# A new instruction order for a fused state-space and gated-MLP kernel: six idle matmuls fewer, all reloads on one queue

## The chip, the cores and the metric

The kernel runs on one core of a Trainium2 chip. The core has five engines that run their own instruction lists and wait for each other by semaphores: TensorE (PE, with its weight loads listed as PEld), VectorE (DVE), ScalarE (ACT), GpSimd (POOL) and SyncE (SP), which here only issues transfers; ACT and POOL issue a few too. Operands lie in SBUF, matmuls write to eight PSUM banks. The metric is the device time of one execution in microseconds (us), lower is better. Of the kernel before there are three timed runs, with a median of 218.31, and one profiled execution.

## The reference

The input is one sequence x of 2048 tokens by 512 channels. After a layer norm over the channels, two branches work on the same normed xn, and the result is x plus both.

```python
xn = layernorm(x)                                   # over D = 512, no gain
# branch A: per channel d a long convolution, its filter from 128 complex modes
dt = exp(log_dt)[:, None]
P  = exp(dt * (A_re + 1j*A_im))[:, :, None] ** l    # l = 0..2047
K  = einsum("dn,dnl,dn->dl", C, P, dt * B).real     # filter, D x 2048
y  = irfft(rfft(pad(xn.T)) * rfft(pad(K)))[:, :2048].T + xn * Dskip
# branch B: gated MLP, F = 1792
h  = sigmoid(xn @ w_gate) * (xn @ w_up)
return x + y + h @ w_down
```

The positions l are rounded to bf16 in the reference, and the kernel follows that.

## The kernel before

**Stages.** The 2048 tokens are 16 tiles of 128 rows. Tile by tile the layer norm takes statistics (DVE, lines 535 to 537, or ACT, lines 528 to 530, by the table `ON_ACT`), POOL takes the power for 1/sqrt (line 491), and DVE or ACT applies it (549, 544). The first four tiles are transposed on PE with the identity (line 558) and evicted to `xnT` (line 293); the other twelve go out to memory and come back by a transposing DMA.

Branch B runs in four groups of 512 tokens. For each of 14 blocks of F there are four gate matmuls (line 1020), a sigmoid on ACT (1029), four up matmuls (1035) and a product on DVE (1050). `UEV` lists the products for which ACT first copies the up projection out of PSUM (line 1046, `us_sb`); for the others DVE reads PSUM. Then four times 14 down matmuls (1079).

Branch A makes powers of the modes (ACT 649, DVE 658 and 660, cast on the way by POOL's DMAs, 654), and from them, for four chunks of 128 channels, two tables by complex multiplies (DVE 715 to 721, ACT 768 and DVE 773 and 774). A chunk's tables are multiplied on PE (799), evicted (the helper `copy`, on ACT as line 293 or on DVE as line 291, by `ON_DVE`), re-sorted on PE (820), evicted to the filter table and given the skip weight (DVE 832). Meanwhile xn goes through a first transform (PE 677) to scratch memory `z_scr`. Then, in two passes over half of the channels and, in each, four pairs of frequency units: reload of z, second transform (PE 868), filter spectrum (PE 883), products (DVE 888 and 892), in the second pass sums (899 to 903), the inverse transform's first half (PE 915 in the first pass, 925 in the second), eviction, store to `v_scr`. `v_scr` is three tensors: all units of pass 0 (`v_scr_97`), units 0 to 5 of pass 1 (`v_scr_98`) and units 6 and 7 of pass 1 (`v_scr_99`), so that each can be reloaded as soon as it is whole. Each is reloaded in four parts, for token tiles 0 to 3, 4 to 7, 8 to 11 and 12 to 15. The inverse transform's second half (PE 988) gives y of a tile, and DVE adds it to x plus the MLP's result (1003), or, for the last group, adds x to the sum that PE made of both (1099). The result is stored two tiles at a time.

A correction for rounded positions, the skip-row terms, is made by small steps (PE 947, DVE 952 to 959, PE 965, ACT 967), stored to `r_scr`, and added to two rows of x by POOL's accumulating DMAs (1066). POOL's line 1116 adds x to finished MLP tiles by DMA.

**What sets the order.** Nothing is ordered at run time: every piece of work is added to a plan (`pl.add`) with an engine, a cost, dependencies and a priority, and the list `ORDER`, written out in the file, says in which sequence the 981 pieces are emitted. Each engine runs its part of that sequence strictly in order; a piece that waits holds back all that follow on its engine. SP's transfers are pieces of that list as well, and one that waits holds back the later ones. PSUM banks and small buffers are dealt out along the same sequence.

**Around the change.** Before the first data PE runs idle matmuls on a zeroed tile, `keep_warm` (line 513): one block of eight and three blocks from `WARM`. The first loads are tiles 0 to 3 of x, log_dt and A (`l_pa`), the identity (`l_id`), B and C (`l_pbc`), then the weights. The reloads of `v_scr` are issued by SP, but for two of the last tensor:

```python
lds.append(dma("ACT" if n == 2 and t % 4 else "SP", vall[16 * u0:16 * u1, t // 2, p], v_v[t // 2],
               deps=v_st[n] + table_free + z_free * p, prio=20 + n + 0.01 * t, pkt=2048, hv=0.9)(64 * KB * (u1 - u0)))
```

Of the kernel before, what the change touches and what calls it, by code (L numbers as in the profile page):

```python
# [13 lines left out]
ACT = mybir.ActivationFunctionType  # L14
# [35 lines left out]
WARM = (4, 4, 3)  # L50
# [17 lines left out]
KB = 1024  # L68
# [114 lines left out]
def _consts():  # L183
# [22 lines left out]
UEV = (2, 4, 5, 7, 11, 13, 14, 15, 16, 17, 18, 19, 23, 24, 25, 28, 29, 30, 31, 32, 33, 34, 35, 36, 37, 38, 39, 40, 41, 42, 43, 44, 47, 53, 54, 55,)  # L206
ON_DVE = (95, 96, 97, 109, 118, 194, 232, 242, 375, 376, 379, 495, 508, 513, 598,)
ON_ACT = (3, 6, 8, 9, 10, 11,)
ORDER = [
# [42 lines left out]

class _Op:
    __slots__ = ("alt", "tab", "eng", "cost", "fn", "prio", "acq", "rel", "dma", "left", "users", "ready", "start", "done", "seq", "mode")
# [69 lines left out]
def kernel(  # L324
# [39 lines left out]
    ident = const.tile([128, 128], BF, name="ident")  # L364
# [811 lines left out]
```

## Time and profile before

| | |
|---|---|
| timed runs | 218.31 us median (217.55 to 221.57) |
| profiled execution | 218.46 us |
| its span, first to last instruction | 216.6 us |
| PE busy | 203.7 us, 94% |
| DVE busy | 196.2 us, 91% |
| ACT busy | 177.7 us, 82% |
| POOL busy | 33.7 us, 16% |
| moved by DMA | 42.40 MB, mean 196 GB/s |
| granted PE clock | 1.00 |

Matmuls overlap in their records, so PE's busy time says that it works, not how well. In a group, busy over count is what one instruction adds, since the mean duration also holds the overlap with the next. The end of an instruction's idle time is put down to what released it.

### The profile page before, as it was taken

What the parts mean: (1) busy time and instruction counts of PE and PEld (TensorE: products, weight loads), DVE (VectorE), ACT (ScalarE), POOL (GpSimd) and SP (SyncE); (2) the same over time, 40 slices, a digit from 0 to 9 for tenths busy, and PEclk for the clock granted to TensorE, in tenths of its full rate; (3) what the DMA queues carried; (4) which work ended last, traced back from release to release, by engine and by line L of the source; (5) the groups of instructions that cost most, each with busy time, mean ns of one, the idle gap of its engine ahead of it and who ended that gap; (6) DMA issues with size and microseconds to landing.
All of it is one profiled execution on the core that took longest, in us unless ns stands there. A gap on an engine that the chain in (4) does not pass through costs nothing.

```text
span 216.6 us, 5697 instructions
## 1 busy us (share of the span) xinstructions
PE 203.7 (94%) x2202; PEld 103.3 (48%) x2228; DVE 196.2 (91%) x433; ACT 177.7 (82%) x365; POOL 33.7 (16%) x63
## 2 busy tenths in 40 slices
PE   7899999999999999999999999999979999998593
PEld 2474444443443454445556555644544555433252
DVE  4899899999999999999999999999869999991484
ACT  4799999999999999899999999975668999960000
POOL 3200543563110231000000006100000005100000
PEclk9999999999999999999999999999999999999999
DMA  5999907995659841596448464915974879689844
GB/s 165 387 413 425 293 5 120 189 129 145 97 194 233 226 140 59 124 268 198 125 160 258 132 207 88 173 40 166 322 232 131 267 247 297 110 248 254 211 172 178
DMA packets 41757, 42.40 MB, mean 196 GB/s; under 512 B 8953, under 2 KB 35202, under 8 KB 41602
## 3 DMA queue, kind: packets, MB, share of 16 engines
q1 hardware_dynamic: 36978, 36.98, 55.5%
q0 software_dynamic: 4512, 4.73, 14.1%
q10 hardware_dynamic: 240, 0.33, 0.6%
q8 instruction: 17, 0.28, 0.5%
q14 instruction: 10, 0.08, 0.1%
HBM read 25.24 MB, written 12.07 MB: 172 GB/s over the span
## 4 chain that ended last, share of the span: by engine, by line
PE 38%; DVE 28%; ACT 24%; DMA 4%; issue 3%; POOL 0%; DVEq 0%; SPq 0%; ACTq 0%; POOLq 0%
PE bank L1020 8%; ACT big L293 8%; PE bank L883 7%; PE bank L1035 7%; DVE hT_sb L1050 5%; PE bank L1079 4%; DVE big L715 4%; DVE big L716 4%; ACT hT_sb L1029 3%; PE bank L513 3%; ACT big L649 3%; DMA big<-v_scr 2%; ACT us_sb L1046 2%; ACT big L544 2%; PE bank L868 2%
## 5 line engine op out<-in xcount | busy, mean ns | idle before, releaser
L293 ACT ACTIVATE big<-bank 128x512 bf16<-128x512 f32 (+2 forms) x149 | 82.7, 688 | 9.3 <-PE bank L799 3.8
L1020 PE MATMUL bank<-xnT,wg_sb 128*128 128x512 bf16 (+1 forms) x237 | 53.1, 361 | 2.0 <-ACT xnT L293 0.6
L1035 PE MATMUL bank<-xnT,wu_sb 128*128 128x512 bf16 x211 | 53.5, 379 | 0.5
L1079 PE MATMUL bank<-wd_sb,hT_sb 128*128 128x512 bf16 (+1 forms) x232 | 49.9, 366 | 0.4
L1029 ACT ACTIVATE hT_sb<-bank 128x512 bf16<-128x512 f32 x56 | 35.1, 687 | 1.4 <-PE bank L1020 1.3
L1020 PEld LDWEIGHTS <-wg_sb 128*128 128x128 bf16 x244 | 23.4, 98 | 25.8 <-issue 4.0
L1079 PEld LDWEIGHTS <-hT_sb 128*128 128x128 bf16 x238 | 22.8, 98 | 25.4 <-issue 1.9
L1035 PEld LDWEIGHTS <-wu_sb 128*128 128x128 bf16 x224 | 20.7, 98 | 27.0 <-issue 4.3
L715 DVE TENSOR_TENSOR big<-big 128x1024 bf16<-128x1024 bf16 (+4 forms) x40 | 26.6, 666 | 0.1
L716 DVE TENSOR_TENSOR big<-big 128x1024 bf16<-128x1024 bf16 (+4 forms) x40 | 26.5, 662 | 0.0
L1046 ACT ACTIVATE us_sb<-bank 128x512 bf16<-128x512 f32 x36 | 24.8, 721 | 0.8 <-DVE hT_sb L1050 0.8
L888 DVE TENSOR_TENSOR big<-big 128x2048 bf16<-128x2048 bf16 x16 | 19.4, 1218 | 0.1
L883 PE MATMUL bank<-big 128*128 128x256 bf16 x160 | 19.3, 273 | 0.0
L883 PEld LDWEIGHTS <-big 128*128 128x128 bf16 x160 | 15.3, 98 | 4.1 <-issue 0.8
L654 POOL DMA_DIRECT2D big<-big x24 | 13.0, 546 | 25.5 <-DVE big L660 25.3
L720 DVE TENSOR_TENSOR big<-big 128x512 bf16<-128x512 bf16 (+4 forms) x40 | 16.4, 410 | 0.0
L721 DVE TENSOR_TENSOR big<-big 128x512 bf16<-128x512 bf16 (+4 forms) x40 | 16.4, 409 | 0.0
L293 ACT ACTIVATE big<-big 128x256 bf16<-128x256 bf16 x33 | 16.3, 527 | 0.0
L768 ACT ACTIVATE sq_sb<-big 128x256 bf16<-128x256 bf16 (+2 forms) x20 | 14.9, 747 | 1.1 <-DVE big L721 1.1
L1050 DVE TENSOR_TENSOR hT_sb<-hT_sb,us_sb 128x512 bf16<-128x512 bf16 x36 | 14.9, 417 | 0.6 <-ACT us_sb L1046 0.5
L1050 DVE TENSOR_TENSOR hT_sb<-hT_sb,bank 128x512 bf16<-128x512 bf16 x20 | 13.3, 679 | 0.0
L1003 DVE TENSOR_TENSOR big<-bank,glu_sb 128x512 bf16<-128x512 f32 x8 | 5.0, 682 | 8.4 <-PE bank L988 8.4
(96 smaller groups left out, 219.8 us busy)
## 6 DMA issues: line engine op xcount, KB each, us to landing
big<-c_E SPq DMA_DIRECT2D x16, 320.0 KB, 4.2
z_scr<-big SPq DMA_DIRECT2D x16, 256.0 KB, 3.1
big<-z_scr SPq DMA_DIRECT2D x16, 256.0 KB, 5.2
v_scr<-big SPq DMA_DIRECT2D x16, 256.0 KB, 2.9
big<-big POOLq DMA_DIRECT2D x24, 128.0 KB, 2.8
big<-in_A_u_dram SPq DMA_DIRECT2D x4, 512.0 KB, 10.3
big<-v_scr SPq DMA_DIRECT2D x4, 512.0 KB, 4.4
wu_sb<-in_B_w_up_dram SPq DMA_DIRECT2D x2, 896.0 KB, 10.1
```

What stands on the lines that cost most here:

```text
L293: nc.scalar.activation(out=get(out), in_=get(in_), func=ACT.Identity)
L715: V.tensor_tensor(out=wide(outp), in0=wide(lo), in1=mre, op=ALU.mult)
L716: V.tensor_tensor(out=wide(tb()), in0=wide(lo), in1=mim, op=ALU.mult)
L720: V.tensor_tensor(out=outp[:, :, 0], in0=outp[:, :, 0], in1=tb()[:, :, 1], op=opr)
L883: T.matmul(bank(sk[kt == NKT - 1])[:, DW * c:DW * c + DW], es()[:, c, kt, :], kT[p][:, kt, :], start=kt in (0, NKT - 1), stop=kt >= NKT - 2)
L888: V.tensor_tensor(out=pp()[:, :, 0:4, :], in0=xx()[:, :, 0, :].unsqueeze(2).to_broadcast([128, 2, 4, DW]), in1=kb().unsqueeze(1).to_broadc ...
L1020: T.matmul(bank(sl)[:, c0:c1], w_at(w, CUT_G, kt, k), xnT[:, grp, kt, c0:c1], start=(kt == 0), stop=(kt == KT - 1))
L1029: S.activation(out=hT_sb[:, hs.idx, k % 2, :], in_=bank(sl), func=ACT.Sigmoid)
L1035: T.matmul(bank(sl), w_at(wu_sb, CUT_U, kt, k), xnT[:, grp, kt, :], start=(kt == 0), stop=(kt == KT - 1))
L1046: S.activation(out=us_sb[:, us.idx, :], in_=bank(sl), func=ACT.Identity)
L1050: V.tensor_tensor(out=h(), in0=h(), in1=us_sb[:, us.idx, :] if on else bank(sl), op=ALU.mult)
L1079: T.matmul(bank(po)[:, 0:c[1] - c[0]], hT_sb[:, hts[k // 2].idx, k % 2, jj * 128:(jj + 1) * 128], wd_sb[:, k, c[0]:c[1]], start=first and ...
```

## The change

Four edits, and what follows from the last. The identity is loaded ahead of `l_pa` in SP's queue. The first block of idle matmuls has nine instead of eight, and of the three further blocks (4, 4, 3) two remain (2, 2). All reloads of `v_scr` are issued by SP. `ORDER` is replaced throughout, and with it the tables that say which engine does a piece: `UEV` has 37 entries for 36, `ON_DVE` 16 for 15, `ON_ACT` five for six. The computation is the same.

```diff
-WARM = (4, 4, 3)
+WARM = (2, 2)
...
-UEV = (2, 4, 5, 7, 11, 13, 14, 15, 16, 17, 18, 19, 23, 24, 25, 28, 29, 30, 31, 32, 33, 34, 35, 36, 37, 38, 39, 40, 41, 42, 43, 44, 47, 53, 54, 55,)
-ON_DVE = (95, 96, 97, 109, 118, 194, 232, 242, 375, 376, 379, 495, 508, 513, 598,)
-ON_ACT = (3, 6, 8, 9, 10, 11,)
+UEV = (0, 1, 3, 10, 12, 15, 16, 18, 19, 20, 21, 22, 24, 25, 26, 27, 28, 29, 30, 31, 32, 33, 34, 35, 36, 37, 38, 39, 40, 41, 42, 44, 46, 48, 49, 54, 55,)
+ON_DVE = (94, 95, 96, 108, 117, 180, 190, 193, 382, 498, 531, 540, 597, 599, 871, 873,)
+ON_ACT = (2, 4, 8, 11, 15,)
 ORDER = [
-    0, 24, 25, 2, 22, 21, 1, 3, 4, 7, 34, 26, 29, 6, 5, 8, 10, 35, 36, 37, 43, 44, 30, 31, 20, 27, 38, 28, 32, 40, 41, 23,
+    1, 28, 21, 22, 29, 2, 0, 3, 23, 24, 33, 4, 7, 6, 30, 34, 25, 35, 42, 43, 39, 20, 31, 32, 26, 27, 45, 36, 40, 44, 41,
...
+    l_id = load("SP", ident[:], cten["ident"].ap(), 32 * KB)
     l_pa = load("SP", par[:, 0:3, :], A_par[:, 0:3, :], 384 * KB, pkt=3072)
-    l_id = load("SP", ident[:], cten["ident"].ap(), 32 * KB)
...
-    warm = [keep_warm(8, -10)]
+    warm = [keep_warm(9, -10)]
...
-            lds.append(dma("ACT" if n == 2 and t % 4 else "SP", vall[16 * u0:16 * u1, t // 2, p], v_v[t // 2],
+            lds.append(dma("SP", vall[16 * u0:16 * u1, t // 2, p], v_v[t // 2],
```

In the emitted programs the new order shows at these places, among others. All 13 idle matmuls stand ahead of the first transposes; before it was 16 and then 3. In the last chunk of the filter (the last 128 of line 799), PE's work between lines 799 and 820 was 12 matmuls of line 1020 and 4 of 1035, and is 8, 4 and 16 of line 868; the four evictions there were one on ACT and three on DVE, and are all on ACT; between lines 820 and 883 there were 16 of line 868, 4 of line 1020 and 8 of line 947, and are 4 of line 1035. After the last 16 of line 925 PE had 8 matmuls of line 1035 and 28 of line 1079 ahead of the first line 988, and has 12 of line 1035, 4 of line 965, 4 of line 1020 and the 28. Line 988 then came as 12, 14 of line 1079, 22, and comes as 16, 14 of line 1079, 18. SP's end of the list is, before and after (tile parts by their first pair of tiles):

```
before: store 99, store 99, reload 98 t2, 98 t4, 99 t4, 98 t0, 99 t0, 98 t6      ACT: 99 t2, 99 t6
after:  reload 98 t4, store 99, store 99, reload 98 t2, 98 t6, store r_scr, 99 t4, 99 t6, 99 t2, 98 t0, 99 t0
```

82 rows, old and new, of the table ORDER are left out of this document.

## The prediction

> **What bounds the kernel now.** First the page's busy shares, then the same in six stretches cut where the kind of work changes. The columns of the second are the stretch, its length, and the busy time (with the instruction count) of PE, PE's weight loads, DVE, ACT and POOL, then the granted clock, the DMA share and GB/s.
>
> ```profile
> span 216.6 us, 5697 instructions
> ...
> PE 203.7 (94%) x2202; PEld 103.3 (48%) x2228; DVE 196.2 (91%) x433; ACT 177.7 (82%) x365; POOL 33.7 (16%) x63
> ```
>
> ```profile
> 0.00:27.00 27.00, 24.31 (x129) 12.72 (x132) 21.91 (x54) 22.58 (x42) 6.28 (x19) 1.00 0.95 337
> 27.00:151.87 124.87, 123.29 (x1407) 60.78 (x1422) 123.97 (x287) 119.17 (x251) 23.97 (x40) 1.00 0.63 151
> 151.87:163.20 11.33, 9.85 (x255) 6.24 (x256) 8.61 (x23) 7.43 (x15) 0.00 (x0) 1.00 0.83 260
> 163.20:191.32 28.12, 27.54 (x290) 13.94 (x292) 27.78 (x47) 26.38 (x55) 3.46 (x4) 1.00 0.78 219
> 191.32:203.11 11.79, 8.91 (x56) 3.93 (x59) 4.08 (x9) 2.17 (x4) 0.00 (x0) 1.00 0.95 246
> 203.11:216.60 13.49, 9.80 (x74) 5.67 (x70) 9.81 (x17) 0.00 (x0) 0.00 (x0) 1.00 0.50 177
> ```
>
> DVE is the bound: from 27 to 151.87 it idles 0.90 us, from 163.20 to 191.32 0.34 us. It loses time in four places: the head, 151.87 to 163.20 (2.72 idle, the last filter chunk's way through PE and ACT), 191.32 to 203.11 (7.71, the store and reload of the last products) and the end (3.68, from the first of the final adds at 203.11). PE has few holes either. So a new order can gain only by less DVE work or by closing those four.
>
> **The change, part by part.** The profiled run took 218.46 us, span 216.6 plus 1.86 around it; the median shown is 218.31. I work from 218.46. Where I count instructions, they are those of the two programs as built, each at busy time over count of its group.
>
> *Head.* These are rows of the chain of waits and of the timeline.
>
> ```profile
> 1.46 6.20 PE bank L513 x16
> 6.39 0.63 ACT L595 ACTIVATE big<-big 128x512 bf16<-128x512 bf16 x1 [0.40 <-DMA big<-in_A_par_dram]
> 7.92 1.09 ACT L293 ACTIVATE xnT<-bank 128x512 bf16<-128x512 bf16 x2 [0.90 <-PE bank L558]
> 8.76 0.81 PE L513 MATMUL bank<-glu_sb 128*128 128x512 bf16 x3
> 2.13 0.43 SPq L427 DMA_DIRECT2D big<-in_A_par_dram  x1
> 2.60 0.43 SPq L427 DMA_DIRECT2D ident<-c_ident  x1
> ```
>
> WARM drops seven idle matmuls, but the first block grows from 8 to 9: six fewer, 13 for 19. Of the 16 ahead of the first transposes three go, and the three behind them. The three ahead cost at most 0.81, so the transposes, which ACT waits 0.90 for, start some 0.65 earlier, if the identity is there, and it is issued 0.47 earlier. The price is the parameter load, now behind it: line 595 waits for that, starts 0.47 later and ends near 7.5, so ACT's 7.92 becomes 7.5 and no less. A gain of 0.4 on ACT; DVE gets part of it, since it also waits for the exponential. Bounds 0 and 0.65; I take **-0.3**. The three behind the transposes run in a hole that ends with ACT's evictions: nothing.
>
> *Work on DVE.* Groups of instructions by line and shape (count, then busy us and mean ns):
>
> ```profile
> L1050 DVE TENSOR_TENSOR hT_sb<-hT_sb,us_sb 128x512 bf16<-128x512 bf16 x36 | 14.9, 417 | 0.6 <-ACT us_sb L1046 0.5
> L1050 DVE TENSOR_TENSOR hT_sb<-hT_sb,bank 128x512 bf16<-128x512 bf16 x20 | 13.3, 679 | 0.0
> L535 DVE BATCH_NORM_STATS2 stats<-big 128x6 f32<-128x512 bf16 x10 | 6.9, 687 | 2.9 <-DMA big<-in_A_u_dram 2.9
> L536 DVE BATCH_NORM_AGGREGATE mv<-stats 128x2 f32<-128x6 f32 x10 | 1.8, 182 | 0.3
> L537 DVE TENSOR_SCALAR ln_ve<-mv 128x1 f32<-128x1 f32 x10 | 1.5, 154 | 0.3
> L291 DVE CAST big<-bank 128x512 bf16<-128x512 f32 x4 | 2.7, 687 | 0.2 <-PE bank L925 0.2
> ```
>
> One tile's statistics move from ACT to DVE: 0.69 + 0.18 + 0.15 = 1.02. One gated product more reads a copy (0.41) and one fewer reads PSUM (0.67): -0.25. Line 291 takes three more 512-wide evictions (2.7/4 = 0.68 each, 2.03), loses three of 328 and gains one of 384. In all DVE gets about 1.8 us more, and ACT is rid of the like. Where it lies decides: up to the last complex multiply of chunk 3 (line 721) only the statistics and the changed product, **+0.77**; after the last sum (line 901) two PSUM products and one eviction more, 1.33 + 0.68 = 2.0, and these fall into the 7.71 hole, at nothing. Ahead of the last sum DVE's work is therefore as before within 0.2. If that hole closes for another reason, the 2.0 come back.
>
> For 27 to 151.87 the orders differ throughout, with the same work but for the 0.77. With 0.90 idle at most 0.9 can be gained; what a worse interleaving loses no row shows, and the head's idle share (27 - 21.91 = 5.09, of which 2.9 is the first load) is the nearest. Bounds -0.9 and +2; I take **+0.4**.
>
> *The last chunk, 151.87 to 163.20.* Timeline rows:
>
> ```profile
> 156.28 0.49 DVE L291 CAST big<-bank 128x328 bf16<-128x328 f32 x1
> 156.95 0.81 PE L820 MATMUL bank<-big,sw 128*32 128x96 bf16 x57
> 159.00 0.27 PE L820 MATMUL bank<-big,sw 128*32 128x96 bf16 x7 [1.24 <-issue]
> 161.00 2.36 PE L883 MATMUL bank<-big 128*128 128x256 bf16 x20
> 163.20 1.23 DVE L888 TENSOR_TENSOR big<-big 128x2048 bf16<-128x2048 bf16 x1
> ```
>
> Line 820 waited for an eviction that DVE did late (156.28, behind a product). After the change ACT does all four, and the filler on PE ahead of line 820 loses four of 16 projection matmuls (0.9, at 0.23 each by the 6.21 us of 27 quoted below) and gains the 16 short ones of line 868: it starts between 0 and 0.9 earlier, say 0.35. In the middle of its 64 matmuls PE stood 1.24 us with nothing to wait for. The 1.24 lie after 57 of the 64; that instruction's place in PE's program falls after the change after 51 of the same 64, since only 12 instructions went ahead of it. So I let the pause recur. Then line 883 stood behind 16 of line 868, 4 projection matmuls and 8 of line 947; 1.73 us in all (159.27 to 161.00); now 4 projection matmuls (0.9) lie between. Gain 0.8, and most of the 0.35 goes into the pause. DVE's own work here falls 0.46, but it waits anyway: **-0.85**. Bounds: 0, and 2.72, all the idle time.
>
> *163.20 to 191.32.* DVE has one copy product and two PSUM products fewer, one eviction and the seven small instructions of the skip-row terms more, -0.46 in all; PE four matmuls fewer (-0.9). Both are over 97% busy, so the smaller counts: **-0.4**. Bounds -0.9, and +0.6 since the DMA share is already 0.78.
>
> *Tail.* Chain, timeline and DMA-issue rows:
>
> ```profile
> 192.09 1.57 ACT L293 ACTIVATE big<-bank 128x512 bf16<-128x512 f32 x3 [1.28 <-PE bank L925]
> 193.69 3.55 DMA v_scr<-big
> 197.65 4.92 DMA big<-v_scr
> 193.68 6.21 PE L1079 MATMUL bank<-wd_sb,hT_sb 128*128 128x512 bf16 x27
> 202.66 1.49 PE L988 MATMUL bank<-big 128*64 128x512 bf16 x12 [2.77 <-DMA big<-v_scr]
> 207.65 2.48 DVE L1003 TENSOR_TENSOR big<-bank,glu_sb 128x512 bf16<-128x512 f32 x4 [0.87 <-PE bank L988]
> big<-v_scr SPq DMA_DIRECT2D x2, 128.0 KB, 4.5
> big<-v_scr ACTq DMA_DIRECT2D x2, 128.0 KB, 5.8
> big<-v_scr SPq DMA_DIRECT2D x4, 384.0 KB, 6.6
> ```
>
> The last products' way (store 3.55, reload 4.92) stays. The two reloads that ACT issued took 5.8 against 4.5 on SP; on SP they cost one issue slot (about 0.5) each, the first wanted is issued first, and one 384 KB reload that stood ahead now goes ahead of the last stores. Of the four last evictions, which begin at 192.1, two are now on DVE (0.68 each) and two on ACT, for three on ACT in a row (1.57): about 0.15 sooner. PE's 2.77 us hole gets eight projection matmuls (1.7) and line 965's, which stood ahead: harmless, and paid for above. After the reload the order puts 16 of line 988 in a row ahead of the 14 down-projection matmuls, for 12: DVE's 0.87 gap goes. Bounds: 0 and 1.6; I take **-1.0**.
>
> Sum: -0.3 + 0.77 + 0.4 - 0.85 - 0.4 - 1.0 = -1.38, so 218.46 - 1.4 = **217.1**.
>
> **Rivals.** *The pause does not recur* at line 820. For it: nothing in the profile names its cause. Against: its place hardly moves. The gain there becomes 2.1: 215.8.
>
> *Every bound on the good side:* 2.72 and 0.9 idle go, the tail gives 1.6: -0.3 + 0.77 - 2.72 - 0.46 - 0.46 - 0.9 - 1.6, 212.8. Against it: six things must agree.
>
> *Slower: the skip-row terms come last.* These rows are of before:
>
> ```profile
> 178.72 0.28 SPq L427 DMA_DIRECT2D r_scr<-big  x1
> 181.39 0.81 POOL L1066 DMA_DIRECT2D big<-r_scr  x1 [45.02 <-ACT big L293]
> big<-in_A_u_dram POOLq DMA_DIRECT2D x2, 256.0 KB, 5.4
> ```
>
> The store of r_scr was 13 us ahead of the last sums; now it stands on SP behind the last two stores (ready by 193.6) and two 384 KB reloads, at some 0.45 us an issue: 194.9. POOL's line 1066 waits for it (181.39 - 178.72 = 2.67), and one 256 KB accumulation of line 1116 stands on POOL behind the two of line 1066 (0.81 each). So that is issued near 199.2 and lands at 204.6. DVE's seventh add needs it: the first add at 202.4 + 0.45, six of 0.62, 206.6. If r_scr's store takes the 6.6 of the reloads ahead of it, the accumulation lands at 208.5, and DVE, in order, stands 1.9 us with all later adds behind it. It decides from 2.0 us of delay on. With 1.9: 219.0.
>
> *Slower: PE's clock.* The 16 idle matmuls took 6.20, 0.39 each, while the three later ones took 0.81 together, and the granted clock is 1.00 in every stretch: the early ones ran at half the pace. What follows:
>
> ```profile
> 10.15 5.39 PE L1020 MATMUL bank<-xnT,wg_sb 128*128 128x256 bf16 x43 [0.58 <-ACT xnT L293]
> 14.92 1.28 ACT L1029
> ```
>
> At the early pace the 43 gate matmuls would end up to 5.4 later, at 20.9; ACT's sine chain and its table load last until 16.2 and hide what its first gates need, not the up-projections behind: 2 us late as a guess between 0 and 4.7, 219.1. [...]
>
> *The tail does not shorten*, because the store and the reload alone set it, and DVE's gap reappears: 218.1.
>
> **How the numbers follow.** Forecast 0.44, no pause 0.18, all good 0.08, skip-row terms 0.18, clock 0.04, tail unchanged 0.08. The range goes from 214.0 (between the two faster rivals) to 220.4 (the slower ones plus the +2 bound of the middle stretch in part). 2% of 218.31 is 4.4 us, about what a measurement of this kernel tells from no change: faster is below 213.9, slower above 222.7. The first holds most of the all-good case, the second needs two slower rivals at once: 0.09, 0.84, 0.07.
>
> **What would show it.** Line 293's first xnT eviction at about 7.5; DVE's busy sum near 198; line 820 to line 888 of the last chunk under 6 us where 163.20 - 156.95 = 6.25 were, with or without an "issue" gap of about 1.2; no PE hole over 1 us ahead of the first line 988; no wait of DVE for a POOL transfer in the last 13 us. I am wrong if DVE's idle time between 27 and the last chunk grows by over 2 us, or if the seventh of the final adds waits.

## The result and the profile after

After the change the kernel takes 216.82 us (median of 20 runs, 214.4 to 220.75); beside it the kernel before took 219.82 (20 runs, 217.23 to 221.79). The ratio is **0.9868, 95% interval 0.9832 to 0.9904**: 1.3% faster. The profiled execution took 216.45 us with a span of 214.4, against 218.46 and 216.6. Forecast from these were 217.1, or -1.4; measured -2.0. Two of the profiled executions of the experiments below (six output buffers, 16 idle matmuls) were among the long ones of their kernel; from those only the place and the cause of a wait is read, not a time.

The page of the kernel after, and its windows at the same events as those of before (columns as there):

```profile
span 214.4 us, 5718 instructions
...
PE 205.0 (96%) x2222; PEld 102.8 (48%) x2222; DVE 197.2 (92%) x437; ACT 176.9 (83%) x360; POOL 37.4 (17%) x63
```

```profile
0.00:27.00 27.00, 24.05 (x128) 12.56 (x129) 22.05 (x53) 22.49 (x41) 5.40 (x17) 1.00 0.90 329
27.00:151.37 124.37, 123.59 (x1420) 60.55 (x1418) 123.92 (x291) 118.44 (x248) 27.83 (x41) 1.00 0.61 155
151.37:161.71 10.34, 8.82 (x244) 5.47 (x242) 8.07 (x17) 7.22 (x15) 1.72 (x2) 1.00 0.84 196
161.71:189.58 27.87, 27.54 (x297) 13.95 (x294) 27.43 (x52) 25.97 (x52) 0.00 (x0) 1.00 0.85 252
189.58:200.69 11.11, 11.09 (x68) 4.77 (x69) 5.90 (x12) 2.75 (x5) 1.78 (x3) 1.00 0.96 250
200.69:214.40 13.71, 9.89 (x74) 5.53 (x70) 9.81 (x17) 0.00 (x0) 0.70 (x1) 1.00 0.55 178
```

DVE is still the bound, with 1.0 us more work in 2.2 us less span. Between 27 us and the last chunk it now idles 0.45 us (0.90 before). The fifth row is new: PE is busy for 11.09 of 11.11 us where it was for 8.91 of 11.79.

For the comparison of many runs I use five events, each the start of an instruction on DVE: the last complex multiply of chunk 3 (line 721), line 888 of the last chunk, the last sum (line 901), the first final add (line 1003) and the last one (line 1099). The first column is a time, the others are distances from the event to the left, in us.

| Profiled run | Line 721 | to 888 | to 901 | to 1003 | to 1099 |
|---|---|---|---|---|---|
| before | 151.53 | 11.66 | 27.70 | 12.21 | 10.27 |
| after | 151.04 | 10.67 | 27.44 | 11.53 | 10.41 |
| difference | -0.49 | -1.0 | -0.26 | -0.68 | +0.14 |

So four of the five distances shrink, and the last grows a little. First the head of the kernel after, in its timeline:

```profile
6.99 0.85 PE L558 MATMUL bank<-ident,big 128*128 128x128 bf16 x8
7.41 0.63 ACT L595 ACTIVATE big<-big 128x512 bf16<-128x512 bf16 x1 [1.11 <-DMA big<-in_A_par_dram]
7.95 1.07 ACT L293 ACTIVATE xnT<-bank 128x512 bf16<-128x512 bf16 x2
8.07 0.69 DVE L597 TENSOR_TENSOR big<-big 128x512 f32<-128x512 bf16 x1 [0.69 <-ACT big L595]
```

The transposes do start 0.5 earlier, but line 595, which waits for the parameter load, starts at 7.41 instead of 6.39, ACT's first eviction at 7.95 instead of 7.92, and DVE waits 0.69 for line 595. In this execution the head gave nothing.

The last chunk's way through PE, same view:

```profile
155.74 0.14 PEld L868 LDWEIGHTS <-m 64*32 64x32 bf16 x16 [0.60 <-DMA big<-z_scr]
156.29 0.74 PE L820 MATMUL bank<-big,sw 128*32 128x96 bf16 x52
158.24 0.31 PE L820 MATMUL bank<-big,sw 128*32 128x96 bf16 x12 [1.21 <-issue]
161.71 1.23 DVE L888 TENSOR_TENSOR big<-big 128x2048 bf16<-128x2048 bf16 x1
```

The pause is there, after the 52nd matmul (after the 57th before), and line 888 follows line 820 by 5.42 us (6.25 before). Line 820 starts at 5.25 behind line 721 (5.42 before), now behind a reload of z_scr.

The tail:

```profile
193.45 0.38 SPq L427 DMA_DIRECT2D r_scr<-big  x1
194.10 6.21 PE L1079 MATMUL bank<-wd_sb,hT_sb 128*128 128x512 bf16 x28
198.91 1.58 POOL L1066 DMA_DIRECT2D big<-r_scr  x2 [41.53 <-DMA big<-v_scr]
199.94 1.46 POOL L1116 DMA_DIRECT2D big<-in_A_u_dram  x1
200.24 1.92 PE L988 MATMUL bank<-big 128*64 128x512 bf16 x16
202.00 9.71 SPq L427 DMA_DIRECT2D out_dram<-big  x9
205.37 1.29 DVE L1003 TENSOR_TENSOR big<-bank,big 128x512 bf16<-128x512 f32 x2 [1.01 <-DMA out_dram<-big]
```

PE's 2.77 us hole ahead of line 988 is gone. But POOL's line 1066 now starts 5.46 us after the store of r_scr (2.67 before), POOL's last accumulation goes out only at 199.94, and DVE's seventh add waits 1.01. The row puts this down to an out store, which would mean an output buffer (there are three); the forecast's slower rival put it down to POOL. The runs decide it.

### The profile page after: what moved, and what is told of

The parts are those of the page before. It is cut to its first block, busy times and chain, and to the rows that moved or that the text cites. A ratio compares the mean times of both kernels' runs of the same rounds, so it can differ in the third digit from the quotient of the medians.

```text
span 214.4 us, 5718 instructions
## 1 busy us (share of the span) xinstructions
PE 205.0 (96%) x2222; PEld 102.8 (48%) x2222; DVE 197.2 (92%) x437; ACT 176.9 (83%) x360; POOL 37.4 (17%) x63
## 4 chain that ended last, share of the span: by engine, by line
PE 43%; ACT 24%; DVE 19%; DMA 8%; issue 2%; SPq 1%; DVEq 0%; ACTq 0%
PE bank L1035 10%; PE bank L1020 10%; PE bank L1079 7%; PE bank L883 6%; ACT big L293 5%; DMA big<-z_scr 4%; ACT hT_sb L1029 4%; ACT big L649 4%; DVE big L715 3%; PE bank L915 3%; DVE big L716 3%; ACT us_sb L1046 3%; DMA big<-in_A_par_dram 2%; DVE big L721 2%; DVE big L720 2%
## 5 line engine op out<-in xcount | busy, mean ns | idle before, releaser
L1020 PE MATMUL bank<-xnT,wg_sb 128*128 128x512 bf16 (+1 forms) x244 | 54.7, 362 | 0.4 <-ACT xnT L293 0.2
L1035 PE MATMUL bank<-xnT,wu_sb 128*128 128x512 bf16 x224 | 54.5, 379 | 0.3 <-ACT us_sb L1046 0.2
L1079 PE MATMUL bank<-wd_sb,hT_sb 128*128 128x512 bf16 (+1 forms) x238 | 50.5, 367 | 0.1
L1029 ACT ACTIVATE hT_sb<-bank 128x512 bf16<-128x512 f32 x56 | 36.3, 689 | 2.4 <-PE bank L1020 2.3
L1020 PEld LDWEIGHTS <-wg_sb 128*128 128x128 bf16 x244 | 22.9, 98 | 24.8 <-issue 3.8
L1046 ACT ACTIVATE us_sb<-bank 128x512 bf16<-128x512 f32 x37 | 25.5, 727 | 0.6 <-DVE hT_sb L1050 0.6
L293 ACT ACTIVATE big<-big 128x256 bf16<-128x256 bf16 x33 | 17.1, 541 | 0.2 <-PE bank L799 0.2
L1050 DVE TENSOR_TENSOR hT_sb<-hT_sb,bank 128x512 bf16<-128x512 bf16 x19 | 12.6, 679 | 0.0
L649 ACT ACTIVATE big<-big 128x1024 f32<-128x1024 f32 x11 | 11.9, 1085 | 0.0
```

Of the source, the lines that this page charges most:

```text
L293: nc.scalar.activation(out=get(out), in_=get(in_), func=ACT.Identity)
L1020: T.matmul(bank(sl)[:, c0:c1], w_at(w, CUT_G, kt, k), xnT[:, grp, kt, c0:c1], start=(kt == 0), stop=(kt == KT - 1))
L1029: S.activation(out=hT_sb[:, hs.idx, k % 2, :], in_=bank(sl), func=ACT.Sigmoid)
L1035: T.matmul(bank(sl), w_at(wu_sb, CUT_U, kt, k), xnT[:, grp, kt, :], start=(kt == 0), stop=(kt == KT - 1))
L1046: S.activation(out=us_sb[:, us.idx, :], in_=bank(sl), func=ACT.Identity)
L1050: V.tensor_tensor(out=h(), in0=h(), in1=us_sb[:, us.idx, :] if on else bank(sl), op=ALU.mult)
```

## The experiments

Each was timed beside the kernel before on the same chip; "ratio" is to that. The expectation of the run with three edits names leads of a packet; the paragraph on the pause explains them.

**The changed kernel again**, unaltered.

> The changed kernel itself, unaltered, as the yardstick of the runs beside it: 1.0 to 1.7% under the kernel before (the 20 runs gave 0.987), the last line 721 near 151.0, line 888 of the last chunk 10.7 us behind it, the last final add 21.9 us behind the last sum. If those three move by more than 0.3 us without an edit, differences of that size in the other runs mean nothing.

Measured: ratio 0.9868 (0.9806 to 0.993), line 721 at 150.94, then 10.08, 27.44, 11.53, 10.99. The first, third and fourth repeat within 0.1. The second doesn't: the pause was 0.80 instead of 1.21. Nor does the last: the seventh add waited 1.51, and the last add came 22.52 behind the last sum, where it was 21.94 in the first execution and 22.48 before the change. The head differs as well: line 595 started at 6.18, and DVE lost its time at a later instruction of line 597, which waited for the second parameter load (B and C, landed 7.0 us after its issue instead of 5.6):

```profile
6.18 0.63 ACT L595 ACTIVATE big<-big 128x512 bf16<-128x512 bf16 x1
11.03 1.29 DVE L597 TENSOR_TENSOR big<-big 128x512 f32<-128x512 bf16 x2 [0.67 <-DMA big<-in_A_par_dram]
```

**The parameter load ahead of the identity matrix**, as before the change.

```diff
-    l_id = load("SP", ident[:], ...)
     l_pa = load("SP", par[:, 0:3, :], A_par[:, 0:3, :], 384 * KB, pkt=3072)
+    l_id = load("SP", ident[:], ...)
```

> The parameter load issued ahead of the identity matrix again, everything else as changed. Theory (the head's term had the wrong sign: what ACT and DVE wait for there is the parameter load, the identity is early enough in either order): line 595 starts at 6.4 to 6.9 in place of 7.41, DVE's 0.69 us wait at line 597 falls to 0.2 or less, and the work behind moves up by 0.4 to 0.7 through to the last line 721 (150.4), since DVE is the bound all the way: 0.2 to 0.3% faster than the changed kernel. Rival (the head's cover is elsewhere): the identity now lands later, the transposes start at 7.5 instead of 6.99, ACT's first xnT eviction comes at 8.4, and the last line 721 stays at 151.0 within 0.2.

Timeline of this run, then its waits of DVE (total, times, longest):

```profile
6.27 0.63 ACT L595 ACTIVATE big<-big 128x512 bf16<-128x512 bf16 x1 [0.34 <-DMA big<-in_A_par_dram]
6.92 1.23 ACT L293 ACTIVATE xnT<-bank 128x512 bf16<-128x512 bf16 x2
6.98 0.68 DVE L597 TENSOR_TENSOR big<-big 128x512 f32<-128x512 bf16 x1
155.19 0.86 PE L820 MATMUL bank<-big,sw 128*32 128x96 bf16 x64
```

```profile
DVE big L1003 <- DMA out_dram<-big: 2.5, 1, 2.5
```

Line 721 came at 150.11, 0.9 ahead of the changed kernel, DVE waited for no parameters, and PE ran through the 64 matmuls without a pause: line 888 followed at 9.10. All of that, 2.5 us at the first final add, reached the end only as 1.0: the adds took 11.89 instead of 10.41, because the seventh now waited 2.49. Ratio 0.9858 (0.9815 to 0.9902), which can't be told from 0.9868. The theory holds in the profile, but a later wait takes the gain.

**The identity first in the kernel before**, the same two lines swapped there.

> The kernel before with the identity matrix ahead of the parameter load, nothing else. By the prediction's step: the transposes wait for the idle matmuls anyway, so they don't move (7.50), line 595 starts 0.47 later (6.9 in place of 6.39), and nothing behind it is late. By what the changed kernel showed (7.41 in place of 6.39): line 595 starts near 7.4, DVE waits 0.5 to 0.7 more at line 597, and the last line 721 comes 0.4 to 0.7 later than 151.53: 0.2 to 0.3% slower than before.

```profile
8.36 0.63 ACT L595 ACTIVATE big<-big 128x512 bf16<-128x512 bf16 x1 [2.22 <-DMA big<-in_A_par_dram]
9.02 0.69 DVE L597 TENSOR_TENSOR big<-big 128x512 f32<-128x512 bf16 x1 [1.65 <-ACT big L595]
```

In the timeline line 595 starts 2.0 later than before, and line 721 comes at 152.50, 0.96 later. Ratio 1.0054 (0.9998 to 1.011): slower by the median, but not quite told apart from no change. Both ways round, the swap costs 0.6 to 1.0 us at line 721 (the pair with POOL's order changed, below, gives 150.71 against 150.02); programs that are equal up to there lie up to 0.33 apart. One pair shows no cost: with the narrow idle matmuls, below, line 721 came at 150.38 with the identity first and at 150.52 without. In the first of these DVE waited only 0.17 for parameters, in the second it waited longer for x (3.6 in all, 3.2 in the first). Over all 14 runs DVE waited 0.2 to 1.7 us for a parameter load, or for line 595 behind it, in each of the nine with the identity first, and for none in the other five.

**16 idle matmuls ahead of the transposes** in the changed kernel.

```diff
-    warm = [keep_warm(9, -10)]
+    warm = [keep_warm(12, -10)]
```

> The changed kernel with the first block of idle matmuls at 12 instead of 9, so that 16 stand ahead of the first transposes as before the change. By the prediction's step (0.3 of the head is theirs): the transposes start at 7.5 to 7.7 instead of 6.99, ACT's first xnT eviction at 8.3 to 8.5 instead of 7.95, the last line 721 up to 0.3 later. Rival (ACT and DVE wait for the parameter load, not for PE): first xnT eviction and the last line 721 move by less than 0.2. The six instructions more at the start of PE's program move the pause in line 820 up by three of its matmuls, to behind the 48th or 49th.

Ratio 0.9811 (0.9683 to 0.9938, four runs), too wide to tell anything of the three. In the profile ACT's first eviction waits 0.97 for the transposes and starts at 8.28: with three idle matmuls more PE is the later one there, and not the parameter load, so the step had the right waiter for this part. The pause was after the 49th matmul, as expected from its place in PE's program:

```profile
156.37 0.73 PE L820 MATMUL bank<-big,sw 128*32 128x96 bf16 x49
158.79 0.35 PE L820 MATMUL bank<-big,sw 128*32 128x96 bf16 x15 [1.69 <-issue]
```

**One tile's statistics back on ACT** in the changed kernel.

```diff
-ON_ACT = (2, 4, 8, 11, 15,)
+ON_ACT = (2, 4, 8, 10, 11, 15,)
```

> One tile's layer-norm statistics (the tenth) go back from DVE to ACT in the changed kernel; DVE loses 1.02 us, ACT gets about 2.0 (a pass of 0.65, one of 0.72, two read-outs of 0.2 and one of 0.3). Theory (as the prediction priced it: DVE has next to no idle time there, so its work counts in full): the last line 721 comes 0.7 to 1.0 us earlier (150.0 to 150.3), 0.3 to 0.5% faster than the changed kernel. Rival (ACT, 118.4 busy of 124.4, hands its results over later, and DVE's idle time of 0.45 grows): the last line 721 stays at 150.9 to 151.2. The run of the changed kernel again put it at 150.94, so 0.2 can be told.

Windows of this run, cut at 27 us and just behind the last complex multiply:

```profile
0.00:27.00 27.00, 24.30 (x131) 12.77 (x132) 22.70 (x54) 23.10 (x42) 5.39 (x17) 1.00 0.88 328
27.00:152.50 125.50, 124.32 (x1417) 60.58 (x1415) 122.69 (x287) 119.51 (x252) 27.47 (x41) 1.00 0.60 153
```

The waits are those from 27 to 152.5 us:

```profile
DVE big L660 <- ACT big L649: 0.7, 1, 0.7
DVE big L773 <- ACT sq_sb L768: 0.7, 1, 0.7
DVE big L715 <- ACT big L293: 0.5, 1, 0.5
DVE hT_sb L1050 <- ACT us_sb L1046: 0.3, 1, 0.3
DVE hT_sb L1050 <- ACT hT_sb L1029: 0.3, 1, 0.3
```

Up to line 721 DVE is busy 145.4 us instead of 146.0 (the sums of the two rows, here and in the kernel after), but idles 7.1 instead of 5.4, 2.81 of it behind 27 us where 0.45 were. Line 721 comes at 152.16, **1.1 later** than in the changed kernel, not 0.7 to 1.0 earlier; ratio 0.9958 (0.9908 to 1.0009). The forecast's reading, that DVE's work counts in full because DVE hardly idles, falls, and so does the rival's "no change". ACT, 95% busy there in the kernel after (118.4 of 124.4), hands DVE its operands: the waits of this stretch above are all for ACT, and the same view of the kernel after lists none. So 1.7 us more on ACT (142.6 for 140.9) came with 1.7 more of idle time on DVE, where its work fell by 0.6. (This is in an order of work made for the statistics on DVE; what they would cost in the order of before was not tried.)

**Six output buffers** instead of three.

```diff
-    pl = _Plan(dict(..., vs=2, ot=3, ...))
+    pl = _Plan(dict(..., vs=2, ot=6, ...))
-    TAIL = dict(ot=32 * KB, glu=38 * KB, xt=46 * KB)
+    TAIL = dict(ot=OFF["W0"], glu=38 * KB, xt=46 * KB)
```

> Six output buffers for the final adds instead of three, in memory that is free by then; nothing else. Theory (the seventh add waited for the first of three output buffers, whose store was issued at 202.0 and landed 3.2 us later instead of the median 2.0): DVE's 1.01 us wait at line 1003 goes, the last line 1099 comes 20.9 to 21.2 us behind the last sum in place of 21.94, 0.3 to 0.5% faster. Rival (it waited for POOL's accumulation of line 1116, issued at 199.94 behind the late r_scr store, landing 4.3 later): the wait stays at 0.8 to 1.0, and the time with it. A third: the wait goes, but DVE then waits for PE, whose last 28 down-projection matmuls (3.23) must end first: 0.3 gained at the most.

The waits of DVE in the tail:

```profile
DVE big L1003 <- DMA big<-in_A_u_dram: 1.8, 1, 1.8
```

The seventh add still waits, 1.8 us, and with no buffer to wait for the profile names the other transfer: POOL's accumulation of line 1116. Ratio 0.985 (0.9786 to 0.9914), as the changed kernel. The output buffer wasn't it.

**POOL's last accumulation first.** Only the order of POOL's three last transfers changes: operation 874 (line 1116) goes ahead of 959 and 960 (line 1066).

```diff
-    ... 608, 965, 962, 959, 960, 874, 796, ...
+    ... 608, 965, 962, 874, 959, 960, 796, ...
```

> POOL's last accumulation of line 1116 goes ahead of the two of line 1066, which wait for r_scr; nothing else moves. Its evictions are done by 154.6, so it can be issued 40 us before DVE's seventh add. Theory (the seventh add waited for this accumulation, queued on POOL behind the late r_scr store): DVE's wait of 1.0 to 1.5 us at the seventh add goes. PE, idle for 0.65 us between 200.24 and the end of its work, then sets the end, so the last line 1099 comes 21.2 to 21.5 us behind the last sum in place of 21.94 to 22.5: 0.2 to 0.5% faster than the changed kernel. Rival (it waited for an output buffer): the wait stays. Second rival: the accumulation, now among the transfers of 155 to 161, where the DMA share is 0.84, makes the last chunk's reloads later by up to the 4.3 it takes to land, and line 888 comes over 11 us behind the last line 721.

POOL's timeline and DVE's in the tail:

```profile
156.40 1.52 POOL L1116 DMA_DIRECT2D big<-in_A_u_dram  x1
198.26 1.60 POOL L1066 DMA_DIRECT2D big<-r_scr  x2 [40.35 <-DMA big<-v_scr]
203.17 1.29 DVE L1099 TENSOR_TENSOR big<-bank,big 128x512 bf16<-128x512 f32 x2 [0.53 <-issue]
204.38 1.28 DVE L1003 TENSOR_TENSOR big<-bank,big 128x512 bf16<-128x512 f32 x2
```

The accumulation goes out 43 us earlier, the seventh add (204.38) doesn't wait, and the adds take 9.93. The last one comes 21.46 behind the last sum (21.94 in the changed kernel). Ratio **0.9804** (0.9757 to 0.9851). The last chunk didn't suffer from the earlier transfer (10.47 to line 888, with a pause of 1.18). Now the fifth add, of line 1099, waits 0.53. Its row names no releaser, but that add needs the skip-row terms, and the second transfer of line 1066 was issued at 198.79 and took up to 4.3 us, which is 203.1.

**The same with the parameter load first.**

> The same, and the parameter load ahead of the identity. In the run with the parameter load alone everything up to the first final add came 2.5 us earlier than in the changed kernel, but the seventh add stood 2.49 us and left 1.0 of it at the end. Theory: with that wait gone, the last line 1099 comes 10.3 to 10.6 us behind the first final add instead of 11.9, span 211.5 to 212.2, about 1% faster than the changed kernel. Rival: the seventh add's wait is put down to an out store there, and if that is right the wait stays and the span is 213.3.

```profile
span 212.3 us, 5691 instructions
```

Line 721 at 150.02, then 9.82, 27.45, 11.54 and 10.25. Ratio **0.9785** (0.9735 to 0.9835), the median 214.30 us beside 219.18: the lowest of all, 0.8% under the changed kernel by the two ratios, with intervals that just touch. The wait is gone; the adds took 10.25, a little under what was expected; the span is 0.1 over, and a pause of 0.54 came back in line 820.

**Idle matmuls of 128 columns instead of 512**, four for one: 78 more instructions at the start of PE's program, the same columns.

```diff
-            for _ in range(n):
-                T.matmul(bank(wsl), glu_sb[:, 0, 0:128], glu_sb[:, 0, :], start=True, stop=True)
+            for _ in range(4 * n):
+                T.matmul(bank(wsl)[:, 0:128], glu_sb[:, 0, 0:128], glu_sb[:, 0, 0:128], start=True, stop=True)
```

> The 13 idle matmuls of 512 columns become 52 of 128 columns: the same idle columns, 39 more matmuls and 39 more weight loads, 78 instructions more at the start of PE's program. Theory (the 1.2 us pause in line 820 hangs on a place in PE's program, since it lay before and after at the same count of PE instructions while the 64 matmuls around it had shifted): the pause moves 39 matmuls up, from behind the 51st or 52nd of the 64 to about the 13th, or goes away if PE isn't running through short matmuls ahead of that place. If it goes, line 888 of the last chunk comes 9.5 instead of 10.7 us behind the last line 721, and the time falls 0.4 to 0.6%. Rival (the pause belongs to line 820, its form or its operands): it stays behind the 51st to 52nd matmul with 1.2 us, and the time doesn't change.

```profile
155.79 0.86 PE L820 MATMUL bank<-big,sw 128*32 128x96 bf16 x64
```

No pause, and line 888 comes 9.43 behind line 721 as the theory said. Ratio 0.9875 (0.9822 to 0.9929): the time didn't follow, since the seventh add took the gain (its wait was 1.56). And a run without this edit (parameter load first) had no pause either, so this run alone proves little; the section on the pause puts all of them together.

**The three edits together.**

> The three edits together: parameter load ahead of the identity, POOL's last accumulation ahead of line 1066's, and 52 narrow idle matmuls for 13. Theory (the pause in line 820 is PE standing until a 16 KB packet of its own program has come, and its length depends on how far ahead of line 820 that packet starts: 0.8 us ahead it was 1.21 in the changed kernel, 0.9 ahead 0.80, 1.4 ahead 0.54, 2.6 to 3.1 ahead none): with the shift the packet starts 2.5 us or more ahead, line 820 runs through, line 888 of the last chunk comes 9.1 to 9.5 us behind the last line 721 (9.8 with the two edits alone), span 211.5 to 212.0, 1.2% under the changed kernel. Rival (the two edits alone have most of it, and the tail's reloads then end last): span 212.3 as without the shift, the gain of the last chunk comes back as a hole ahead of line 988.

No pause, as expected, but line 820 started 5.93 behind line 721 (5.08 with two edits), because line 868 ahead of it waited 1.28 for a reload of z_scr:

```profile
155.89 0.14 PEld L868 LDWEIGHTS <-m 64*32 64x32 bf16 x16 [1.28 <-DMA big<-z_scr]
156.45 0.86 PE L820 MATMUL bank<-big,sw 128*32 128x96 bf16 x64
```

Line 888 came at 9.95, not 9.1 to 9.5; span 212.4; ratio 0.9815 (0.9746 to 0.9883). The shift adds nothing that can be measured to the two edits: the rival's figure, though the gain was eaten by a reload ahead of line 820 and not by one ahead of line 988.

**The reloads.** First the two 128 KB reloads back on ACT in the changed kernel, then all on SP in the kernel before; nothing else in either.

```diff
-            lds.append(dma("SP", vall[...], ...
+            lds.append(dma("ACT" if n == 2 and t % 4 else "SP", vall[...], ...
```

> The changed kernel with the two 128 KB reloads of the last products back on ACT's queue, as before the change. Theory (the reload sets when the first line 988 can start): they land 5.8 us after issue instead of 4.6, the hole of PE ahead of line 988 is back at 1 to 2 us, and the first line 988 comes 11.7 or more behind the last sum in place of 11.09: 0.2 to 0.5% slower than the changed kernel. Rival (in the changed kernel PE's own 28 down-projection matmuls, 6.21 us, end last there, and r_scr's way sets the end): no change, within 0.2%.

> The kernel before with the two reloads moved from ACT's queue to SP's and nothing else. Theory (this part of the change has a worth of its own): PE's hole of 2.77 us ahead of line 988 shrinks by 0.5 to 1.2 and the time by 0.2 to 0.5%. Rival (on SP the same reloads stand behind others, or the hole is set by the 384 KB reloads): the hole stays at 2.5 to 3.0, the time within 0.2%.

PE in the tail, first in the changed kernel with the reloads on ACT, then in the kernel before with them on SP:

```profile
192.39 6.21 PE L1079 MATMUL bank<-wd_sb,hT_sb 128*128 128x512 bf16 x27
198.52 1.05 PE L988 MATMUL bank<-big 128*64 128x512 bf16 x8
199.90 1.05 PE L988 MATMUL bank<-big 128*64 128x512 bf16 x8 [0.32 <-DMA big<-v_scr]
```

```profile
193.96 6.21 PE L1079 MATMUL bank<-wd_sb,hT_sb 128*128 128x512 bf16 x27
200.27 1.05 PE L988 MATMUL bank<-big 128*64 128x512 bf16 x8
203.44 0.62 PE L988 MATMUL bank<-big 128*64 128x512 bf16 x4 [2.11 <-DMA big<-v_scr]
```

In the changed kernel the reloads' queue hardly matters: the first add is 11.54 behind the last sum on either queue, because PE's own work (28 down-projection matmuls and what stands ahead) ends last. That is the rival's reason. Its time isn't shown: the ratio of 0.9918 (0.9879 to 0.9957) is 0.5% above the changed kernel's, as the theory had it, though the intervals overlap. The tail was slower by 0.3 to 0.9 us than in the two executions of the changed kernel (22.83 from the last sum to the last add), and that is the seventh add again, with 1.42 of wait. In the kernel before, line 988 starts right after the down projection, the hole comes eight matmuls later with 2.11 instead of 2.77, and the last add is 22.12 behind the last sum for 22.48: 0.36 us. The hole shrank by 0.66, as the theory had it; the 0.36 us are under 0.2%, where the rival had put the time, and the ratio of 0.9965 (0.9926 to 1.0005) isn't told apart from nothing.

**The pause in line 820.** All 14 traces show it or its absence. The trace has 17 packets of 16 KB in a queue of the kind "instruction" (page of the kernel after):

```profile
q8 instruction: 17, 0.28, 0.6%
```

PE has 4444 instructions in that page (2222 matmuls and as many weight loads), one packet for some 260; that the queue is PE's is the author's reading of this count, and no trace names the engine. The start of the packet next ahead of line 820, against the start of line 820, and the pause:

| Run | Packet's lead, us | Pause after matmul | Pause, us |
|---|---|---|---|
| 16 idle matmuls | 0.1 | 49 | 1.69 |
| before; all reloads on SP in it | 0.6; 0.4 | 57; 57 | 1.24; 1.19 |
| identity first, in before | 0.8 | 57 | 0.92 |
| POOL's order | 0.5 | 52 | 1.18 |
| after; again | 0.8; 0.9 | 52; 52 | 1.21; 0.80 |
| six output buffers | 1.4 | 52 | 0.42 |
| POOL's order, parameters first | 1.4 | 52 | 0.54 |
| 128 columns; three edits | 2.6; 3.3 | none | none |
| parameters first; reloads on ACT; statistics on ACT | 3.0; 3.1; 3.4 | none | none |

The place moves with the count of PE instructions ahead (three matmuls more, three matmuls sooner), the length roughly with the lead, and where it paused PE went on 2.4 to 2.7 us after the packet's start each time. The reading is that PE stands until a packet of its own program has come, and that line 820, which issues 52 matmuls and as many weight loads in 0.74 us, is where it runs dry. It fits all 14, but no run delayed a packet by itself, so it isn't shown, and what sets a packet's start isn't settled: seven kernels with the same list of PE instructions gave leads from 0.5 to 3.4. The packets start all through the run (from 21.8 to 201.4 us in the kernel after).

## Why the prediction was right, and where not

The direction and the range held (217.1, 214.0 to 220.4; measured 216.8), the size was short (-1.4, for -2.0 in the profiled execution and 1.3%, or 2.9 us, by the ratio), and it came out of terms of which several were wrong and partly cancelled. That the sum came so near was in part luck.

**Head, forecast -0.3: wrong in sign.** The step that failed is "line 595 waits for that, starts 0.47 later". With one issue of 0.47 ahead of it the line started 1.0 later in the changed kernel and 2.0 later in the kernel before, and where it was on time, in the repeat, DVE waited 0.67 for the next parameter load instead. Undone, the identity's part gave 0.7 to 0.9 at line 721 in two pairs of runs and nothing in a third; done alone it cost 0.96. What the three idle matmuls are worth wasn't resolved.

**Work on DVE, +0.77, and the middle, +0.4: wrong in sign, together.** At line 721 the forecast sum with the head was +0.87, measured -0.49. If the identity's part costs 0.6 to 1.0, the other two came to about -1.3 instead of +1.17. The step that failed is that DVE's work there counts in full because DVE idles 0.90 only. With one tile's statistics on ACT DVE was busy 0.6 less and came 1.1 later. The instructions were counted rightly, but the busy time up to line 721 grew by only 0.1 (145.88 to 145.97, from the first two rows of each table of windows), as the instructions overlapped more: their own times add up to 170.8 and 171.9 us, 1.1 more, and their overlap grew from 25.2 to 26.1. What the order alone gives in the middle stays open, since it could not be changed apart from its tables.

**Last chunk, -0.85: right**, -1.0 measured, with the mechanism in each part, though the size hangs on a pause that the forecast let recur without a cause (the same kernel gave -1.6 in the repeat): the pause recurred, after the 52nd where the 51st was forecast; line 820 started earlier (0.17, half the 0.35) and line 883 came sooner. The chance of 0.18 for "the pause does not recur" had a cause that the forecast couldn't see: five of the 14 runs had none, and line 888 then came 9.1 to 9.5 behind line 721 where nothing else was late.

**163 to 191, -0.4: mis-sized**, -0.26, and 27.43 to 27.45 in all eleven runs of the new order.

**Tail, -1.0: half right**, -0.53, and in the repeat nothing (22.52 from the last sum to the last add, 22.48 before). PE's hole closed as forecast, and the first add came 0.68 sooner; "DVE's 0.87 gap goes" failed: that gap went, and one of 1.01 came at the seventh add. That is the slower rival, in its place and by its mechanism (the late store of r_scr, POOL's queue, the accumulation of line 1116), at half the price it was given (1.9; 0.8 to 2.5 in the other runs that show it). It was put at 0.18 and as an alternative to the forecast; it came with it. The forecast named the seventh add's wait as a sign that it was wrong, and on the tail it was. The reloads' queue, which the term leaned on, matters little: 0.36 alone in the kernel before, nothing that can be told in the new order.

**The clock**, the rival with the early pace, didn't come. The granted clock can't show that: it stands at 1.00 in the first row as well, where the 13 idle matmuls of the kernel after started 0.40 to 0.43 us apart, and the last of the kernel before 0.22. The gate matmuls show it: the first 40, of 256 columns, took 272 ns each in both kernels. What sets the early pace no run shows, so the 0.04 for this rival was the author's estimate.

Taken one at a time, the reloads give 0.9965 and the identity 1.0054, so that the order with its tables is worth about 0.985 (0.9868 / 0.9965 / 1.0054). That is an estimate: it holds if the parts add up, and neither of the two is told apart from 1 by its interval. By it the order is the part that pays; by the profiles the identity's place takes some of it back, and POOL's order hides more.

## What to carry to other kernels

A gain upstream is worth what the next fixed event lets through: the seventh add waited for a transfer whose issue stood behind a late store on another queue, and 2.5 us gained ahead of it became 1.0 at the end until POOL's last transfer was moved ahead of that wait. Put on a queue behind a late wait only what needs that wait. And a bound engine with next to no idle time isn't proof that work taken off it helps: look at who hands it its operands, and how full that engine is.

## What the runs showed of the hardware

- **With a small load ahead of it on the queue a larger one came late and unevenly.** Line 595, which waits for the parameter load, started at 6.0 to 6.4 in the five runs with that load first, and at 6.2 to 8.4 in the nine with the 32 KB identity first, though it is issued only 0.47 later. Why it varies so isn't shown.
- **A small store close behind large reloads took longer.** The 8 KB store of r_scr released POOL 2.4 to 4.3 us after its issue in the three runs of the old order (2.67 before the change), and 4.8 to 5.9 in the eleven of the new one, right behind two reloads of 384 KB. No run moved the store alone.
- **TensorE stood up to 1.7 us waiting for nothing that the profile names**, in a run of short matmuls, when a 16 KB packet of the queue of the kind "instruction" had started 1.4 us or less ahead of that run, and not when it had started 2.6 us or more ahead.
- **For the same wait the rows of different runs named different releasers.** At the seventh add it was an out store (1.01 us, kernel after), PE (1.42, reloads on ACT) or POOL's accumulation (1.8, six output buffers); more output buffers and POOL's order settled it, the row didn't.
